# Expert 0 of a recurrent attention layer with a top-2 mixture of experts: four low halves made earlier, a third bank for turned rows, high and low halves in one tile, three scatters issued apart

## Chip, cores and metric

One core of a Trainium2 chip runs the whole program. The metric is the device time of one execution in microseconds (us), the median of three runs.

## What is computed

Four batches of eight heads and 768 steps go through a gated linear recurrence with a running maximum. Its output, 3072 rows of 320 numbers, is the input x of eight experts, of which each row goes to two:

```python
noisy_logits = x @ w_gate + log1p(exp(x @ w_noise)) * noise
top2_w = softmax over the two largest
for e in range(8):
    for k in range(2):
        mask = top2[:, k] == e
        h = np.maximum(x[mask] @ w1[e], 0.0)           # 320 -> 1024
        out[mask] += top2_w[mask, k, None] * (h @ w2[e])   # 1024 -> 320
```

## The kernel before

**Precision.** Each matrix is kept as a high half (rounded to fp32r) and a low half (what the rounding left). A product is three matmuls: high with high, high with low, low with high. W2H and W2L are the halves of an expert's second weights, HH and HLO those of the first product's result after the relu, XH and XL those of the turned rows.

**Stages.** The recurrence and the routing fill the first 131 us. Then expert 0 is computed while the routing of the last rows still runs on VectorE; its rows are dealt in three parts of 3, 2 and 2 tiles (tiles 0 to 2, 3 and 4, 5 and 6; tile 6 has 64 rows). After it come experts 1 to 7, with whole sets of tiles. For one expert the rows are gathered by POOL with indirect DMAs (gather, line 781), turned by TensorE for experts 0 and 1 (transpose_x, line 807: three transposes into one PSUM bank, then ACT copies to XH at line 813 and VectorE subtracts to XL and XH at lines 814 and 815), multiplied with the first weights (mm1, line 997), then with the second (mm2, line 1029), scaled by VectorE to a tile y, and added to the output in HBM by an indirect DMA of POOL (put, line 1055).

**Order of expert 0 (lines 1096 to 1162).** First product of part 0 in eight steps f, with routing work put in between by advance (line 1074); the low half of each step is held in the list `later` and issued at the end of advance. Then the second product of tiles 0 to 2 in three passes k (line 1113): HH with W2H, HLO with W2H, HH with W2L. In pass 1 VectorE makes the eight low halves W2L at line 1119; a decode and two gathers (rows of tiles 3 and 4) are issued early in pass 1; in pass 2 tiles 3 and 4 are turned. The three results are not scattered yet, they stay in `held`. Then the first product of part 1 (line 1133), in which the last decode and five gathers are issued (tiles 5 and 6 of expert 0, tiles 0 to 2 of expert 1); two more gathers (line 1141), the three held scatters (line 1143), and the second product of tiles 3 and 4 with five turns in between (tiles 5, 6 and, for expert 1, 0 in that of tile 3; tiles 1 and 2 in that of tile 4). Then the first product of part 2 (line 1149) with the turns of tiles 3 and 4 of expert 1 after its steps 0 and 3, and the second product of tiles 5 and 6.

**Banks.** bank (line 733) deals PSUM banks in turn: "h" for first products from s0, s1 and e, "x" for turned rows from s0 and s1, "y" for second products from st and o. s0 and s1 have two buffers each, e, st, o and xt one. A new tile waits for the readers of the one before it in its buffer. Each engine works its instructions in the order in which the program issues them.

**Tail columns.** Where a part has more than 768 columns, its last 64 (tile 6) go to a tile HT of their own: a relu at line 1026 and a low half at line 1027, after the relu and the low half of the other columns (lines 1016 and 1019). That is so for experts 0 to 4.

Of the kernel before, what the change touches and what calls it, by code (L numbers as in the profile page):

```python
# [7 lines left out]
F32 = mybir.dt.float32  # L8
FR = mybir.dt.float32r
# [55 lines left out]
def build(ctx, tc, qk, vk, og, fi, noise, wgn, w1, w2, cst, ce, out):  # L65
# [666 lines left out]

    def bank(use):

        n = dict(h=("s0", "s1", "e"), x=("s0", "s1"), y=("st", "o"))[use]
        turn[use] += 1
        name = n[turn[use] % len(n)]
        return psum.tile([128, 512], F32, name=name, bufs=2 if name in ("s0", "s1") else 1)
# [27 lines left out]
    def weigh(e, h=None):  # L766

        if not h:
            GW[e] = rt.tile([128, 7], F32, name="gw", bufs=2)
            GW[e, 2] = rt.tile([128, 7, 2], F32, name="gw2", bufs=2)  # L770
        t = tiles(e, h)
        n = slice(t[0], t[-1] + 1)
        V.tensor_mul(GW[e, 2][:, n], XG[:, n, DM:DM + 2], KM[:, TC * e + n.start:TC * e + n.stop])
        V.tensor_add(GW[e][:, n], GW[e, 2][:, n, 0], GW[e, 2][:, n, 1])
# [23 lines left out]
    def tiles(e, h=None):  # L798
        if h is None:
            return range(7 if is_long(e) else 6)  # L800
        c = parts(e)[h]
        return range(c.start // 128, -(-c.stop // 128))
# [154 lines left out]
    XTP = XTB[:, 0:384].rearrange("p (j t) -> p j t", j=3)  # L957
    m2 = ctx.enter_context(tc.tile_pool(name="m2", bufs=1, reuse_waits="tile"))
    RAW2 = m2.tile([128, 8, DM], F32, name="raw2")
    HH = m2.tile([128, 8, NM], FR, name="hh")  # L960
    HLO = m2.tile([128, 8, NM], FR, name="hlo")
    HT = m2.tile([128, 8, 128], FR, name="ht")
    XB = m2.tile([128, 12, 224], F32, name="xb")
    XT = m2.tile([128, 3, NT], F32, name="xt_")

# [31 lines left out]
    def mm1(e, h, f, later=None):  # L997
        c, s = parts(e)[h], slice(f * 128, f * 128 + 128)
        n = c.stop - c.start
        ps = bank("h")  # L1000
        hh = [(W1H[:, k, s], XH[:, k, c]) for k in range(2)]
        hl = [(W1H[:, k, s], XL[:, k, c]) for k in range(2)] + [(W1H[:, 2, s], XH[:, 2, c])]
        lh = [(W1L[:, k, s], XH[:, k, c]) for k in range(2)] + [(W1L[:, 2, s], XH[:, 2, c])]

        ops = hh + (hl + lh if e else lh + hl)
        for i, (l, r) in enumerate(ops):
            T.matmul(ps[:, 0:n], l, r, start=i == 0, stop=i == len(ops) - 1)  # L1007
        if e > 1:
            m = NM // 2
            x = ps[:, 0:m].rearrange("p (t x) -> p t x", x=64)  # L1010
            hi, lo = (a[:, f].rearrange("p (t h x) -> p h t x", h=2, x=64)[:, h] for a in (HH, HLO))
        else:
            c = slice(c.start, min(c.stop, NM))
            m = c.stop - c.start
            x, hi, lo = ps[:, 0:m], HH[:, f, c], HLO[:, f, c]
        A.activation(hi, x, AF.Relu)  # L1016

        def rest():
            V.scalar_tensor_tensor(lo, x, 0.0, hi.bitcast(F32), op0=OP.max, op1=OP.subtract)  # L1019

        if later is None:
            rest()
        else:
            later.append(rest)
        if m < n:
            A.activation(HT[:, f, 0:64], ps[:, m:n], AF.Relu)
            V.scalar_tensor_tensor(HT[:, f, 64:], ps[:, m:n], 0.0, HT[:, f, 0:64].bitcast(F32), op0=OP.max, op1=OP.subtract)

    def mm2(e, t, b="y", between={}):
        n = rows_of(t)  # L1030
        ps = bank(b)[:, 0:DM]
        y = m2.tile([128, DM], F32, name="y", bufs=TA + 1)
        if n == 128:
            c = slice(128 * t, 128 * t + 128)
            for j in range(8):
                T.matmul(ps, HH[:, j, c], W2H[:, j], start=j == 0, stop=False)  # L1036
                T.matmul(ps, HH[:, j, c], W2L[:, j], start=False, stop=False)  # L1037
                T.matmul(ps, HLO[:, j, c], W2H[:, j], start=False, stop=j == 7)  # L1038
                if j in between:
                    transpose_x(between[j])  # L1040
        else:

            for j in range(8):
                T.matmul(ps, HT[:, j], W2H[:, j], start=j == 0, stop=False)
                T.matmul(ps, HT[:, j], W2L[:, j], start=False, stop=j == 7)
            A.activation(y[0:n], ps[n:128], AF.Copy)
            V.tensor_add(y[0:n], y[0:n], ps[0:n])
            ps = y
        V.tensor_scalar(y[0:n], ps[0:n], GW[e][0:n, t:t + 1], None, op0=OP.mult)  # L1049
        return y  # L1050
# [4 lines left out]
    def put(e, t, y):  # L1055
        n = rows_of(t)

        P.memset(gap, 0.0)
        st = P.indirect_dma_start(out=out, out_offset=bass.IndirectOffsetOnAxis(ap=token(e, t), axis=0),  # L1059
                                  in_=y[0:n], in_offset=None, compute_op=OP.add)  # L1060
        for o in puts.setdefault(e, []):
            tc.declare_no_dep(st.ins, o.ins, reason="an expert has a token once")
        puts[e].append(st)
# [29 lines left out]

    unit[0] = NU
    weigh(0, 0)
    wipe = lambda: next(clear, None)
    lag[:] = 8, 11
    for f in range(8):
        mm1(0, 0, f, later)
        for _ in range(3):  # L1100
            wipe()
        A.activation(W2H[:, f], raw2[:, f], AF.Copy)
        if f == 0:
            logits(NU)
        if f == 1:
            t_part(NU - 1)
            tc_part(NU - 1)
        if f == 2:
            logits(NU + 1)
        advance(0.85, 4)  # L1110
    lag[:] = 10, 9
    sums = [bank("h")[:, 0:DM] for _ in tiles(0, 0)]
    for k, (l, r) in enumerate(((HH, W2H), (HLO, W2H), (HH, W2L))):
        for n in range(24):
            t, j = divmod(n, 8)
            T.matmul(sums[t], l[:, j, 128 * t:128 * t + 128], r[:, j], start=k == 0 and j == 0, stop=k == 2 and j == 7)
            if k == 1 and n % 2 == 0 and 6 <= n < 22:
                x = n // 2 - 3
                V.tensor_sub(W2L[:, x], raw2[:, x], W2H[:, x].bitcast(F32))
            if n % 2:  # L1120
                wipe()
                advance((0.27, 0.0, 0.27 if n < 14 else 0.0)[k])
            if k == 2 and j == 7:
                held[t] = m2.tile([128, DM], F32, name="y", bufs=TA + 1)
                A.activation(held[t], sums[t], AF.Copy, scale=GW[0][:, t:t + 1])
            if k == 2 and n in (14, 19):
                transpose_x(tiles(0, 1)[n // 19])
# [11 lines left out]
    dealing = deal()  # L1139
    load_w2(1)  # L1140
    gather(1, ts=tiles(0, 1))
    for t in held:
        put(0, t, held[t])
    for t in tiles(0, 1):
        put(0, t, mm2(0, t, "y", {0: 5, 3: 6, 6: 0} if t == 3 else {2: 1, 5: 2}))
    weigh(0, 2)
    gather(1, ts=tiles(0, 2))
    side = split_w1(V)
    for f in range(8):
        mm1(0, 2, f)  # L1150
        next(dealing, None)
        if f == 5:
            next(side)
        if f in (0, 3):
            transpose_x(tiles(0, 1)[f // 3])
    run(dealing)
    for t in tiles(0, 2):
        y = mm2(0, t)
# [212 lines left out]
```

## Time and profile before

| | us |
|---|---|
| median of 3 runs | 531.01 |
| all runs | 529.98, 531.01, 535.59 |
| profiled execution | 529.92 |
| its span, first to last instruction | 528.1 |
| PE (matmul) busy | 507.6 |
| DVE busy | 344.3 |
| ACT busy | 250.2 |
| POOL busy | 227.6 |

PE is TensorE's matmuls, PEld its weight loads, DVE is VectorE, ACT ScalarE, POOL GpSimd. The ends of matmuls are modelled and the next one starts before the last ends, so the step from start to start is what a matmul takes. In square brackets a row names the idle time of its engine before it and what ended it; "issue" is a wait for nothing that the profile shows.

### The profile page before, as it was taken

To read this page: it belongs to the slowest core of one execution; us is meant where nothing else is said; L and a number is where in the kernel's file an instruction comes from. 1 tells how busy PE (TensorE), PEld (TensorE's weight loads), DVE (VectorE), ACT (ScalarE), POOL (GpSimd) and SP (SyncE) were. 2 spreads that over 40 slices of the span, in tenths; PEclk is the share of its full clock that TensorE was granted. 3 is DMA by queue.
4 is the path that set the end of the run, shared out by engine and by line. 5 is a ranking of instruction groups with operands and counts; after the bars stand their busy time and mean duration, and the time that the engine had idled before them with its cause. 6 is when DMAs were issued, how large, how long until landed. Compare 5 with 4: busy or idle time off the path is not lost.

```text
span 528.1 us, 13192 instructions
## 1 busy us (share of the span) xinstructions
PE 507.6 (96%) x5052; PEld 476.8 (90%) x5053; DVE 344.3 (65%) x963; ACT 250.2 (47%) x607; POOL 227.6 (43%) x294
## 2 busy tenths in 40 slices
PE   9899989998999899999999999999999999999994
PEld 4688888887988797999999999999999999999994
DVE  7788989999887377763765485367448447545410
ACT  7688878889513145441533353054325315514300
POOL 7366575264012746245515623460553245141043
PEclk9699999999999899999999999999999999999998
DMA  5697786876767527059329515931862483272033
GB/s 163 185 273 238 218 230 187 230 223 209 256 191 238 96 40 204 18 116 261 87 53 271 101 38 107 262 91 37 235 119 61 102 256 87 59 169 25 2 38 41
DMA packets 52437, 76.80 MB, mean 145 GB/s; under 512 B 10809, under 2 KB 43072, under 8 KB 52368
## 3 DMA queue, kind: packets, MB, share of 16 engines
q1 hardware_dynamic: 40288, 53.20, 33.6%
q0 software_dynamic: 12080, 22.69, 21.3%
q8 instruction: 42, 0.69, 0.5%
q14 instruction: 27, 0.22, 0.1%
HBM read 52.27 MB, written 17.48 MB: 132 GB/s over the span
## 4 chain that ended last, share of the span: by engine, by line
PE 75%; DVE 14%; ACT 4%; issue 3%; POOL 2%; DMA 2%; SPq 0%; POOLq 0%; DVEq 0%
PE s L1007 23%; PE e L1007 11%; PE o L1037 5%; PE o L1036 5%; PE o L1038 5%; PE st L1037 5%; PE st L1036 5%; PE st L1038 5%; PE o L385 3%; DVE p L362 3%; PE s L348 2%; DVE ob L639 2%; PE e L325 2%; PE st L376 1%; DVE kd L356 1%
## 5 line engine op out<-in xcount | busy, mean ns | idle before, releaser
L1059 POOL DMA_INDIRECT y_out<-y,tok x53 | 87.2, 1645 | 191.9 <-DVE y L1049 190.8
L1016 ACT ACTIVATE hh<-s 128x384 fp32r<-128x384 f32 (+3 forms) x91 | 42.8, 470 | 89.7 <-PE s L1007 82.7
L1007 PE MATMUL s<-xh,w1h 128*128 128x384 f32 (+5 forms) x273 | 76.8, 338 | 0.7 <-DVE vc L462 0.7
L781 POOL DMA_INDIRECT xg<-rows,tok x53 | 60.0, 1133 | 28.3 <-issue 14.4
L1019 DVE SCALAR_TENSOR_TENSOR hlo<-s,hh 128x384 fp32r<-128x384 f32 (+3 forms) x91 | 47.8, 525 | 27.0 <-ACT hh L1016 23.3
L1007 PE MATMUL s<-xh,w1l 128*128 128x384 f32 (+5 forms) x273 | 62.4, 336 | 0.7 <-DVE xh L815 0.7
L1037 PE MATMUL o<-w2l,hh 128*128 128x320 f32 x184 | 57.3, 312 | 0.0
L1036 PE MATMUL o<-w2h,hh 128*128 128x320 f32 x184 | 57.2, 311 | 0.0
L1038 PE MATMUL o<-w2h,hlo 128*128 128x320 f32 x184 | 56.6, 307 | 0.0
L1036 PE MATMUL st<-w2h,hh 128*128 128x320 f32 x176 | 55.2, 313 | 0.4 <-issue 0.4
L1037 PE MATMUL st<-w2l,hh 128*128 128x320 f32 x176 | 55.4, 315 | 0.1
L1038 PE MATMUL st<-w2h,hlo 128*128 128x320 f32 x176 | 54.6, 310 | 0.4 <-issue 0.4
L1007 PEld LDWEIGHTS s<-xh,w1h 128*128 128x128 f32 x273 | 48.9, 188 | 2.6 <-PE s L1007 0.9
L1007 PEld LDWEIGHTS s<-xh,w1l 128*128 128x128 f32 x273 | 47.9, 188 | 2.3 <-DVE xh L815 0.9
L1007 PE MATMUL s<-xl,w1h 128*128 128x384 f32 (+5 forms) x182 | 46.3, 336 | 0.0
L1016 ACT ACTIVATE hh<-e 128x384 fp32r<-128x384 f32 (+3 forms) x45 | 21.3, 474 | 45.3 <-PE e L1007 43.1
L1049 DVE TENSOR_SCALAR y<-o,gw 128x320 f32<-128x320 f32 x23 | 12.6, 550 | 43.4 <-PE o L1038 43.4
L1049 DVE TENSOR_SCALAR y<-st,gw 128x320 f32<-128x320 f32 x22 | 12.1, 551 | 43.8 <-PE st L1038 43.7
L397 POOL TENSOR_TENSOR xr<-tm,vk 128x320 f32<-128x320 f32 x24 | 20.9, 871 | 42.2 <-ACT w L328 12.0
L1007 PE MATMUL e<-xh,w1h 128*128 128x384 f32 (+5 forms) x135 | 38.7, 340 | 0.1
L385 PE MATMUL o<-vk,p 104*64 104x41 f32 (+2 forms) x768 | 30.0, 237 | 5.2 <-DVE p L362 2.5
L1036 PEld LDWEIGHTS o<-w2h,hh 128*128 128x128 f32 x184 | 34.6, 188 | 0.2 <-DVE y L1049 0.2
(235 smaller groups left out, 1267.9 us busy)
## 6 DMA issues: line engine op xcount, KB each, us to landing
raw<-w_in SPq DMA_DIRECT2D x7, 1280.0 KB
raw<-w_in SPq DMA_DIRECT2D x7, 1024.0 KB
qk<-qk_in SPq DMA_DIRECT2D x24, 256.0 KB
raw<-w_in SPq DMA_DIRECT2D x19, 256.0 KB
y_out<-zrow SPq DMA_DIRECT2D x15, 320.0 KB
vk<-vk_in POOLq DMA_DIRECT2D x24, 162.0 KB
vk<-vk_in SPq DMA_DIRECT2D x24, 162.0 KB
vk<-og_in SPq DMA_DIRECT2D x24, 160.0 KB
```

The source lines that it names most:

```text
L362: V.tensor_mul(PP[u], SQ[u], W[u])
L385: T.matmul(OQ[u][half[p], h, :], PP[u][n, p, h, :], VK[u % 4][p][n, h * 41:h * 41 + 41], start=True, stop=True)
L397: P.tensor_mul(XR[u], tm.rearrange("p h d -> p (h d)"), SG[u % 4])
L781: P.indirect_dma_start(out=XG[0:rows_of(t), t], out_offset=None, in_=XD[0:n], in_offset=bass.IndirectOffsetOnAxis(ap=token(e, t), axis=0), ...
L1007: T.matmul(ps[:, 0:n], l, r, start=i == 0, stop=i == len(ops) - 1)
L1016: A.activation(hi, x, AF.Relu)
L1019: V.scalar_tensor_tensor(lo, x, 0.0, hi.bitcast(F32), op0=OP.max, op1=OP.subtract)
L1036: T.matmul(ps, HH[:, j, c], W2H[:, j], start=j == 0, stop=False)
L1037: T.matmul(ps, HH[:, j, c], W2L[:, j], start=False, stop=False)
L1038: T.matmul(ps, HLO[:, j, c], W2H[:, j], start=False, stop=j == 7)
L1049: V.tensor_scalar(y[0:n], ps[0:n], GW[e][0:n, t:t + 1], None, op0=OP.mult)
L1059: st = P.indirect_dma_start(out=out, out_offset=bass.IndirectOffsetOnAxis(ap=token(e, t), axis=0), in_=y[0:n], in_offset=None, compute_op= ...
```

## The change

Four edits. (1) The low halves W2L of the chunks 0 to 3 are appended to `later` in steps 4 to 7 of expert 0's first product, those of the chunks 4 to 7 are issued in pass 1 at n = 4, 8, 12, 16 (before: all eight, at n = 6 to 20). (2) Turned rows get their bank from xt, s0, xt, s1 in turn in place of s0, s1. (3) HH, HT and HLO become views of one tile HX, so that the high half of the tail columns lies right behind HH: one relu writes both, and the low half of the tail follows that of the other columns. This holds for all experts. (4) Of the held scatters, tile 0's is issued before the second product of tile 3, tile 1's before that of tile 4, tile 2's after step 1 of the first product of part 2. The two turns in that product move from steps 0 and 3 to steps 2 and 4.

```diff
-        n = dict(h=("s0", "s1", "e"), x=("s0", "s1"), y=("st", "o"))[use]
+        n = dict(h=("s0", "s1", "e"), x=("xt", "s0", "xt", "s1"), y=("st", "o"))[use]
...
-    HH = m2.tile([128, 8, NM], FR, name="hh")
-    HLO = m2.tile([128, 8, NM], FR, name="hlo")
-    HT = m2.tile([128, 8, 128], FR, name="ht")
+    HX = m2.tile([128, 8, 2 * NT], FR, name="hx")
+    HH, HT, HLO = HX[:, :, 0:NT], HX[:, :, NM:NT + CS], HX[:, :, NT + CS:]
...
+            hi, lo = HH[:, f, c], HLO[:, f, c.start:c.start + m]
+            top = x[:, 0:m], hi[:, 0:m]
         A.activation(hi, x, AF.Relu)
 
         def rest():
-            V.scalar_tensor_tensor(lo, x, 0.0, hi.bitcast(F32), op0=OP.max, op1=OP.subtract)
+            V.scalar_tensor_tensor(lo, top[0], 0.0, top[1].bitcast(F32), op0=OP.max, op1=OP.subtract)
+            if m < n:
+                V.scalar_tensor_tensor(HT[:, f, CS:], ps[:, m:n], 0.0, HT[:, f, 0:CS].bitcast(F32), op0=OP.max, op1=OP.subtract)
...
-        if m < n:
-            A.activation(HT[:, f, 0:64], ps[:, m:n], AF.Relu)
-            V.scalar_tensor_tensor(HT[:, f, 64:], ps[:, m:n], 0.0, HT[:, f, 0:64].bitcast(F32), op0=OP.max, op1=OP.subtract)
...
+    def low_w2(x):
+        V.tensor_sub(W2L[:, x], raw2[:, x], W2H[:, x].bitcast(F32))
...
         A.activation(W2H[:, f], raw2[:, f], AF.Copy)
+        if f > 3:
+            later.append(lambda x=f - 4: low_w2(x))
...
-            if k == 1 and n % 2 == 0 and 6 <= n < 22:
-                x = n // 2 - 3
-                V.tensor_sub(W2L[:, x], raw2[:, x], W2H[:, x].bitcast(F32))
+            if k == 1 and n % 4 == 0 and 4 <= n < 20:
+                low_w2(n // 4 + 3)
...
-    for t in held:
-        put(0, t, held[t])
     for t in tiles(0, 1):
+        put(0, t - 3, held[t - 3])
         put(0, t, mm2(0, t, "y", {0: 5, 3: 6, 6: 0} if t == 3 else {2: 1, 5: 2}))
...
+        if f == 1:
+            put(0, 2, held[2])
         if f == 5:
             next(side)
-        if f in (0, 3):
-            transpose_x(tiles(0, 1)[f // 3])
+        if f in (2, 4):
+            transpose_x(tiles(0, 1)[f // 4])
```

## Rows read from the trace of the kernel before

**Rows 1.** Stages of the span: the first column is the stretch in us from the span's start, then its length, the busy time and (instructions) of PE, PEld, DVE, ACT and POOL, the granted clock of TensorE (1.00 is its upper level), the DMA engines' share and GB/s.

```profile
146.30:160.70 14.40, 14.18 (x92) 11.83 (x90) 13.85 (x69) 3.19 (x8) 2.61 (x3) 1.00 0.64 200
...
169.50:182.90 13.40, 11.85 (x65) 9.93 (x64) 3.05 (x9) 2.47 (x6) 10.20 (x12) 0.88 0.51 99
182.90:192.00 9.10, 8.27 (x72) 7.99 (x72) 7.30 (x28) 3.05 (x14) 5.42 (x6) 0.99 0.44 66
...
200.00:224.00 24.00, 24.00 (x130) 21.15 (x129) 17.75 (x47) 11.82 (x30) 10.89 (x15) 1.00 0.39 116
...
477.00:500.00 23.00, 23.00 (x134) 23.00 (x134) 12.23 (x25) 10.86 (x24) 1.67 (x2) 1.00 0.09 13
```

**Rows 2.** The timeline of the end of the first product of part 0 and the start of the second (start, duration, engine, line, operation, out<-in, count, idle time before).

```profile
143.48 0.19 DVE L540 SCALAR_TENSOR_TENSOR co<-t,ue 128x32 f32<-128x32 f32 x1 [0.18 <-ACT t L701]
...
145.98 0.23 DVE L601 TENSOR_SCALAR rk<-rk,bump 128x4 f32<-128x4 f32 x1 [0.82 <-ACT rk L509]
...
149.07 1.42 DVE L639 TENSOR_SCALAR ob<-spot,bi,cs 128x128 f16<-128x128 f16 x6
149.20 1.19 PEld L1116 LDWEIGHTS e<-w2h,hh 128*128 128x128 f32 x8 [0.38 <-DVE hlo L1019]
...
150.78 0.27 PEld L448 LDWEIGHTS <-ob 128*128 128x128 f16 x8
```

**Rows 3.** The same timeline where passes 1 and 2 meet: the eight low halves, the matmuls that wait for them, and the gather of tile 4.

```profile
153.92 3.29 DVE L1119 TENSOR_TENSOR w2l<-raw,w2h 128x320 fp32r<-128x320 f32 x8
...
154.74 3.97 PE L1116 MATMUL s<-w2l,hh 128*128 128x320 f32 x15
...
155.61 1.29 POOL L781 DMA_INDIRECT xg<-rows,tok  x1 [0.30 <-issue]
155.66 0.19 PEld L1116 LDWEIGHTS s<-w2l,hh 128*128 128x128 f32 x1 [0.21 <-DVE w2l L1119]
```

**Rows 4.** The same timeline at the end of pass 2: the turn of tile 4 on PE, its last low half on DVE, and the matmul of the next first product that waits for that.

```profile
159.61 0.49 PE L811 MATMUL s<-cs,xg 128*128 128x128 f32 x3
...
161.74 0.29 DVE L815 TENSOR_TENSOR xh<-s,xh 64x128 fp32r<-64x128 f32 x1
...
162.08 0.39 PE L1007 MATMUL s<-xh,w1l 128*128 128x256 f32 x1 [0.66 <-DVE xh L815]
```

**Rows 5.** PE's timeline in the second product of tiles 3 and 4: its first two matmuls, the turn of tile 5 and the matmul behind it, the turn of tile 6, a matmul after a gap, and the last two.

```profile
169.50 0.31 PE L1036 MATMUL o<-w2h,hh 128*128 128x320 f32 x1
169.64 0.31 PE L1037 MATMUL o<-w2l,hh 128*128 128x320 f32 x1
...
170.02 0.52 PE L811 MATMUL s<-cs,xg 128*128 128x128 f32 x3
170.29 0.39 PE L1036 MATMUL o<-w2h,hh 128*128 128x320 f32 x1
...
171.79 0.40 PE L811 MATMUL s<-cs,xg 64*128 64x64 f32 x3
...
179.74 0.62 PE L1036 MATMUL st<-w2h,hh 128*128 128x320 f32 x1 [0.40 <-issue]
...
182.39 0.47 PE L1037 MATMUL st<-w2l,hh 128*128 128x320 f32 x1
182.66 0.47 PE L1038 MATMUL st<-w2h,hlo 128*128 128x320 f32 x1
```

**Rows 6.** ACT's timeline in the same stretch: the copies of the turned tiles 5 and 6, then DVE's last step on tile 6, then ACT's copies of tiles 0 to 2, three in one row.

```profile
174.03 0.49 ACT L813 ACTIVATE xh<-s 128x384 fp32r<-128x384 f32 x1 [2.44 <-PE s L811]
...
178.34 0.33 ACT L813 ACTIVATE xh<-s 128x192 fp32r<-128x192 f32 x1 [3.82 <-PE s L811]
...
179.01 0.23 DVE L815 TENSOR_TENSOR xh<-s,xh 64x64 fp32r<-64x64 f32 x1
...
181.24 1.25 ACT L813 ACTIVATE xh<-s 128x384 fp32r<-128x384 f32 x3 [2.56 <-remote]
```

**Rows 7.** POOL's timeline in the same stretch: the last of seven gathers, the first and the last of the three held scatters, the scatter of tile 3, and the second of the two gathers behind that of tile 4.

```profile
174.68 1.01 POOL L781 DMA_INDIRECT xg<-rows,tok  x1 [0.30 <-issue]
...
175.99 1.64 POOL L1059 DMA_INDIRECT y_out<-y,tok  x1 [0.19 <-issue]
...
179.81 1.55 POOL L1059 DMA_INDIRECT y_out<-y,tok  x1 [0.19 <-issue]
...
183.35 1.55 POOL L1059 DMA_INDIRECT y_out<-y,tok  x1 [1.86 <-DVE y L1049]
...
188.57 1.00 POOL L781 DMA_INDIRECT xg<-rows,tok  x1 [0.30 <-PE s L1007]
```

**Rows 8.** The first product of part 2: the wait of ACT's tail relu in 182.9 to 192 us (total, times, longest), the low half, tail relu and tail low half of step 0, the first matmul of step 5 after its gap, and the first of the second product behind step 7.

```profile
ACT ht L1026 <- DVE hlo L1019: 3.2, 4, 1.2
...
185.23 0.28 DVE L1019 SCALAR_TENSOR_TENSOR hlo<-e,hh 128x128 fp32r<-128x128 f32 x1
185.55 0.23 ACT L1026 ACTIVATE ht<-e 128x64 fp32r<-128x64 f32 x1 [1.24 <-DVE hlo L1019]
...
185.81 0.22 DVE L1027 SCALAR_TENSOR_TENSOR ht<-e,ht 128x64 fp32r<-128x64 f32 x1 [0.29 <-ACT ht L1026]
...
189.23 0.44 PE L1007 MATMUL s<-xh,w1h 128*128 128x192 f32 x2 [0.74 <-DVE vc L462]
...
191.96 0.33 PE L1036 MATMUL o<-w2h,hh 128*128 128x320 f32 x1
```

More of the change, by code (lines that the diff above doesn't have):

```diff
@@ L1007, in mm1 @@
             T.matmul(ps[:, 0:n], l, r, start=i == 0, stop=i == len(ops) - 1)
+        m = NM // 2 if e > 1 else min(c.stop, NM) - c.start
+        x = ps[:, 0:n]
         if e > 1:
-            m = NM // 2
-            x = ps[:, 0:m].rearrange("p (t x) -> p t x", x=64)
-            hi, lo = (a[:, f].rearrange("p (t h x) -> p h t x", h=2, x=64)[:, h] for a in (HH, HLO))
-        else:
-            c = slice(c.start, min(c.stop, NM))
-            m = c.stop - c.start
-            x, hi, lo = ps[:, 0:m], HH[:, f, c], HLO[:, f, c]
+            x = x.rearrange("p (t x) -> p t x", x=CS)
+            hi = HH[:, f].rearrange("p (t x) -> p t x", x=CS)[:, h:h + 2 * (n // CS) - 1:2]
+            lo = HLO[:, f].rearrange("p (t h x) -> p h t x", h=2, x=CS)[:, h]
+            top = x[:, 0:m // CS], hi[:, 0:m // CS]
+        else:
+            hi, lo = HH[:, f, c], HLO[:, f, c.start:c.start + m]
+            top = x[:, 0:m], hi[:, 0:m]
         A.activation(hi, x, AF.Relu)
         def rest():
-            V.scalar_tensor_tensor(lo, x, 0.0, hi.bitcast(F32), op0=OP.max, op1=OP.subtract)
+            V.scalar_tensor_tensor(lo, top[0], 0.0, top[1].bitcast(F32), op0=OP.max, op1=OP.subtract)
+            if m < n:
+                V.scalar_tensor_tensor(HT[:, f, CS:], ps[:, m:n], 0.0, HT[:, f, 0:CS].bitcast(F32), op0=OP.max, op1=OP.subtract)
         if later is None:
```

## The prediction

> **What bounds the kernel now.** I read the stages of the span first [rows 1]. From 200 to 500 us PE is busy in all of every stretch (the rows show the first and the last of 13): experts 1 to 7 are bound by matmuls that the change doesn't touch, so a shorter tail relu there frees ACT and DVE time that nothing waits for, and I count nothing for it. What can move lies between 146 and 192 us, in expert 0: there PE's row shows gaps, one stage has a granted clock of 0.88, and in the first stage DVE is busy 13.85 of 14.40 us, so it is DVE's order that sets the end there. Then I read the timelines of these stages, for what each engine waits for.
>
> In 146 to 160.7 us DVE makes the eight low halves in one block after the decode, and PE's matmuls of pass 2 come at their pace: each waits about 0.2 us for one [rows 3]. DVE is late by as much behind them, and the next first product waits 0.66 us for the low half of turned tile 4 [rows 4].
>
> In 169.5 to 182.9 us two second products and five turns take 13.4 us [rows 1]. From start to start a matmul takes 0.147 us (169.50 to 169.64) and a turn 0.27 (170.02 to 170.29) [rows 5]: 48 x 0.147 + 5 x 0.25 = 8.3 us, so 5.1 us are lost. The reader is to see that ACT copies turned tile 5 at 174.03 though its turn started at 170.02, tile 6 at 178.34 though its turn started at 171.79, and tiles 0 to 2 together at 181.24 [rows 5, 6]. In the later part PE's matmuls come with gaps that the profile calls issue, and the last run at 0.27 us a step [rows 5], the lower clock level. The three held scatters follow seven gathers without a pause; ACT catches up in the third scatter, which ends at 181.36 [rows 6, 7]. That is a coincidence in time; no row says that one delays the other.
>
> In 182.9 to 192 us eight steps of a first product and two turns take 9.1 us. A step without a gap is 0.91 us (steps 5 to 7 from 189.23 to 191.96), so 8 x 0.91 + 2 x 0.25 = 7.8 us, and 1.3 are lost, most of it ahead of 189.23, where step 5 waits for its bank [rows 1, 8].
>
> **Low halves sooner.** One takes 3.29 / 8 = 0.41 us [rows 3]. Four of them, 1.64 us, move ahead of the decode. DVE had idle time of 0.18 and 0.82 us in steps 4 to 6 [rows 2]; the first moved one fills 0.18 and the second fits in the 0.82 with what the first left over. The third and fourth find none and push what is behind them by 0.82 us: the low half of step 7, on which the bank of the third sum waits (PE goes at 149.20), the OB operands that the burst's weight loads at 150.78 need [rows 2], the decode, and behind it the two gathers. So pass 1 ends some 0.6 us later (between 0.41 and 0.82, as some of it hides in PE's order). Pass 2 no longer waits: from about 155.35, 24 x 0.147 + 2 x 0.25 = 4.0 us, it could end at 159.4 in place of 160.68. What is late next is the gather of tile 4: issued at 156.4, not 155.61. It was landed by 159.61, when the tile was turned [rows 3, 4], so it is landed at the latest 4.0 us after its start, at 160.4; if it had landed earlier than its turn, the new turn is at 159.6 or before. From the turn the chain is 1.75 us: 0.49 each for the turn and its copy, and some 0.8 for two DVE steps, of which the second takes 0.29 [rows 4, 6]. The first product then goes on at 161.35 to 162.2 in place of 162.08: between +0.7 and -0.1, I take **0.5 us gained**. The block behind it, DVE's OB work, ends 0.8 us sooner and doesn't hold this. The weight loads behind the low halves on SP's queue start up to 0.9 us earlier, are needed 30 us later, and meet the two gathers more; that is in the lower bound.
>
> **One tile for both halves.** Before, the tail relu waits for the low half of the other columns (3.2 us in four times), so one step goes through ACT, DVE, ACT and DVE: 185.23 to 186.03 from the first low half on [rows 8]. After, a relu over 192 columns is followed by two DVE steps, 0.28 + 0.22 us; eight instructions of ACT fall away in this stage. The bank comes free about 0.3 us sooner a step, and a turn's copy no longer stands behind a tail relu on ACT's queue.
>
> **Another bank, turns moved.** With the new turn of banks, steps 1, 4 and 5 of this product get buffers that turns 0 and 2 or part 1 left, and step 5 doesn't wait for step 2. Of the 1.3 us I take **1.2 gained** with the edit above; the rest stays in bank e, which has one buffer and is dealt to steps 0, 3 and 6. Bounds 0.5 and 1.3. The other side of this edit is in the stage before: xt has one buffer, and tiles 4, 6 and 1 get it one after another. So the turn of tile 1 now waits until DVE is done with tile 6, which was at 179.24 (179.01 + 0.23) [rows 6]; before, it had a buffer of its own.
>
> **Scatters apart.** Tile 0's scatter keeps its place. Behind it POOL now waits for tile 3's y, behind that come tile 1, tile 4, two gathers and tile 2. POOL gets later by two scatters, 3.7 us (179.81 - 175.99 is two of them [rows 7]), and with it the two gathers behind tile 4's, which ended at 189.57 [rows 7]. Their rows are turned after the second product of tile 5, which starts at 191.96 [rows 8] and takes 24 x 0.147 = 3.5 us; so gathers that end at 193.3 are hidden, with 1 to 2 us to spare for their landing. If the burst of scatters is what holds up PE and ACT, they catch up when the first ends, near 177.6: tile 6 is done at about 178, tile 1 is turned then, and what is left, 15 matmuls and two turns, 15 x 0.147 + 2 x 0.25 = 2.7 us, ends at 180.7, 2.2 us gained. If not, tile 1 waits until 179.24, and the same rest ends at 181.9 at the upper clock level: 1.0 gained, since PE's scattered matmuls of 177 to 180.5 then run in one piece. At the lower level (0.27 a step) it takes 5.0 us and ends at 184.2: 1.3 lost. If everything that was lost goes, 5.1 are gained. I take **1.5 us gained**, between the first two, which are the nearest to the rows.
>
> A rule that speaks against the change bears on this. The clock was granted at 0.88 in this stage [rows 1], and PE had worked with gaps before it fell. The Trainium skill (TensorE: Matmul & The Clock Gate, HAM oscillation — how this bites in real kernels) says that a wait of PE for data can put its clock back to half rate, with the work behind the wait starting cold. By it the waiting turn would cost the 1.3 us above and the sum would be 529.5; by the trace, where the gaps were longer before the clock fell, it is 526.7.
>
> **Sum.** 0.5 + 1.2 + 1.5 = 3.2 us off the profiled execution's 529.92 gives **526.7 us**. That execution lies 1.1 us under the median of 531.01, within the spread of the three runs. A change under 1% (5.3 us) can't be told from none here.
>
> **Rivals.** (a) The delay in 169.5 to 182.9 us goes altogether, since it needs ten indirect DMAs without a pause: 0.5 + 5.1 + 1.3 = 6.9, so 523.0. For it speaks that ACT follows its turns at once where POOL is quiet (159.61 to 160.14 of tile 4); against it that tile 5's copy was already 3.5 us late before the first scatter [rows 6, 7], and the gathers stay. (b) The one buffer of xt takes the place of the burst: tile 6 is read as late as before or later, PE stands until then, and the clock falls. At the old 178.34 this costs 1.3 us, and every us later costs one more; with 1.2 gained behind it and nothing in front, the kernel is slower than before from 178.5 on. With a read one us later it is 529.92 + 2.3 - 1.2 = 531.0; with one at 181.24, as the last three had, 532.9. Against it speaks that the two later scatters are away then. (c) The stage is what it was, since neither scatters nor banks set it: only 0.5 and 1.2 count, 528.2.
>
> **How the numbers follow.** The forecast has 0.45, (a) 0.22, (b) 0.18, (c) 0.15. Under the forecast the time is 525 to 529 by the bounds of its terms. The range reaches from (a) at 523.0 to (b) at 531.0: 522.5 to 531.5, which leaves out the later reads of (b) and about 0.1 on the other side. Faster by over 1% than the median is below 525.7: (a) and a little of the forecast, 0.28. Slower by over 1% needs over 536.3, which only a long wait of (b), or DVE's pushed chain together with it, could give: 0.04. Within 1%: 0.68.
>
> **What would show it.** Pass 2 in one piece without waits for W2L, ending near 159.5 to 160.2; the stall ahead of the first product of part 1 shorter but not gone; ACT's copies of tiles 5 and 6 still late, those of 0 to 2 no longer in one row at 181; the turn of tile 1 behind DVE's last step on tile 6; 169.5 to 182.9 shorter by 1 to 2 us; no gap before step 5 of part 2's product; 24.00 of 24.00 as before from 200 us on. I am wrong if POOL's scatters have no bearing on ACT's late copies, if tile 1's wait for its bank lasts over 3 us, or if the later decode makes the gathers of tiles 3 and 4 the new wait.

## The result and the profile after

The changed kernel takes 534.75 us (median of 20 runs, 529.54 to 540.01) against 531.75 for the one before, measured beside it: a ratio of 1.0053, with a 95% interval of 1.0028 to 1.0078, so some 2.8 us slower (3.0 by the two medians). That is within the 1% named ahead, but on the other side of the forecast, and above its range. The profiled execution takes 534.53 us, its span is 532.8.

Each stage runs from its first matmul to the first matmul of the next. Here are two traces of each kernel, the second ones from the experiments below.

| us | before | before, again | after | after, again |
|---|---|---|---|---|
| first product of expert 0 starts at | 132.99 | 133.47 | 136.30 | 133.05 |
| first product of part 0 | 13.38 | 13.49 | 13.48 | 13.46 |
| three passes | 14.31 | 14.31 | 18.93 | 19.19 |
| first product of part 1 | 8.82 | 8.88 | 9.11 | 9.38 |
| second product of tiles 3, 4 | 13.42 | 11.19 | 11.30 | 10.48 |
| first product of part 2 | 9.04 | 10.08 | 7.75 | 7.75 |
| second product of tiles 5, 6 | 6.65 | 6.67 | 6.66 | 6.66 |
| experts 1 to 7 and end | 329.44 | 329.47 | 329.23 | 329.45 |
| from the first product to the end | 395.1 | 394.1 | 396.5 | 396.4 |

The program up to 133 us is the same in both kernels and takes a different time in each execution, so I compare by stages. From the first product on, the changed kernel loses 1.3 to 2.4 us: 4.6 to 4.9 in the passes, 0.2 to 0.6 behind them, and in the two stages after that it gets back up to 2.9 (in one of the four pairings of these traces it loses 0.1) and 1.3 to 2.3.

The stages of the changed kernel in the view that [rows 1] show of before (same columns):

```profile
149.78:168.71 18.93, 13.56 (x91) 12.33 (x90) 13.93 (x69) 3.19 (x8) 2.33 (x3) 0.90 0.73 225
168.71:177.82 9.11, 9.11 (x73) 9.07 (x73) 5.82 (x31) 3.23 (x8) 2.07 (x3) 0.84 0.28 89
177.82:189.12 11.30, 9.12 (x65) 8.55 (x64) 3.71 (x11) 2.58 (x6) 7.08 (x9) 1.00 0.41 92
189.12:196.87 7.75, 7.75 (x73) 7.75 (x71) 7.26 (x30) 3.83 (x10) 6.77 (x8) 1.00 0.63 83
200.00:224.00 24.00, 24.00 (x128) 20.84 (x128) 18.86 (x47) 12.33 (x27) 12.73 (x17) 1.00 0.47 126
```

PE is busy 13.56 us in the passes, somewhat less than the 14.18 of before, in a stage that is 4.6 us longer: it stands. The timeline of the changed kernel shows where, with the loads of expert 1's weights on SP's queue:

```profile
158.13 1.69 DVE L1098 TENSOR_TENSOR w2l<-raw,w2h 128x320 fp32r<-128x320 f32 x4
158.42 1.10 POOL L781 DMA_INDIRECT xg<-rows,tok  x1 [0.88 <-DVE km L479]
...
158.96 2.37 PE L1122 MATMUL s<-w2l,hx 128*128 128x320 f32 x15
159.49 0.38 SPq L153 DMA_DIRECT2D raw<-w_in  x1
159.82 1.01 POOL L781 DMA_INDIRECT xg<-rows,tok  x1 [0.30 <-issue]
159.97 1.12 SPq L150 DMA_DIRECT2D raw<-w_in  x2
...
161.57 0.55 PE L811 MATMUL s<-cs,xg 128*128 128x128 f32 x3 [0.24 <-DMA xg<-rows,tok]
...
166.94 0.90 PE L811 MATMUL xt<-cs,xg 128*128 128x128 f32 x3 [4.09 <-DMA xg<-rows,tok]
...
168.71 0.63 PE L1006 MATMUL s<-xh,w1h 128*128 128x256 f32 x2
```

Four low halves follow the decode (158.13), not eight, and PE's matmuls of pass 2 come in one row without waiting for one (158.96). But the low halves are the readers of the tile into which expert 1's weights are loaded. So the third of the four, done at about 159.4 (158.13 and three of 0.42), lets the load of line 153 start, 0.33 us ahead of the gather of tile 4 (159.82). The chain of waits names what follows (start, duration):

```profile
159.82 7.07 DMA xg<-rows,tok
```

Before, the same load was issued 1.27 us behind that gather: 156.88 in its timeline, against 155.61 [rows 3], and PE turned tile 4 at 159.61 [rows 4].

```profile
156.88 0.38 SPq L153 DMA_DIRECT2D raw<-w_in  x1
```

The DMA queues of the changed kernel in 161.5 to 162.5, 162.5 to 163.5 and 164.5 to 165.5 us (q0 is POOL's queue, q1 SP's; packets, MB, share of the 16 engines):

```profile
q1 hardware_dynamic: 94, 0.39, 100.2%
...
q1 hardware_dynamic: 100, 0.41, 100.6%
...
q0 software_dynamic: 35, 0.14, 63.6%
q1 hardware_dynamic: 34, 0.08, 35.6%
```

For two us the engines carry nothing but the load; the gather's packets come after it. By 163.5 us the load has moved 0.91 of its 1.05 MB (0.11 MB in the us before these windows, then 0.39 and 0.41). Before, in 157 to 158 and 158 to 159 us, the gather went first:

```profile
q0 software_dynamic: 17, 0.09, 43.6%
...
q1 hardware_dynamic: 28, 0.11, 68.5%
q0 software_dynamic: 31, 0.07, 18.2%
```

A lead at the issue is not yet a lead at the engines. In the 18 traces the first packet of a gather of tile 3 or 4 that nothing held up comes 1.7 to 2.0 us after its issue, and the first of the load 1.0 to 1.4 us after its own. Of the 1.27 us before, about half a us was left: the gather's first packet is at 157.59, the load's at 158.09.

In the second product of tiles 3 and 4 the timeline answers to [rows 5 to 7]:

```profile
178.26 0.51 PE L811 MATMUL s<-cs,xg 128*128 128x128 f32 x3
...
180.03 0.40 PE L811 MATMUL xt<-cs,xg 64*128 64x64 f32 x3
...
180.92 0.49 ACT L813 ACTIVATE xh<-s 128x384 fp32r<-128x384 f32 x1 [1.10 <-PE xt L811]
...
185.24 0.33 ACT L813 ACTIVATE xh<-xt 128x192 fp32r<-128x192 f32 x1 [3.82 <-remote]
...
185.91 0.23 DVE L815 TENSOR_TENSOR xh<-xt,xh 64x64 fp32r<-64x64 f32 x1
...
186.23 0.52 PE L811 MATMUL xt<-cs,xg 128*128 128x128 f32 x3 [2.18 <-ACT xh L813]
```

ACT copies tile 6 at 185.24, 5.2 us after its turn began. The turn of tile 1 waits for xt until DVE is done with tile 6 (186.14; the row names ACT's copy, but that ended at 185.57), as rival (b) has it, but at a clock of 1.00.

### The profile page after: what moved, and what is told of

It reads as the page before. It is cut to its first block, busy times and chain, and to the rows that moved or that the text cites. A ratio compares the mean times of both kernels' runs of the same rounds, so it can differ in the third digit from the quotient of the medians.

```text
span 532.8 us, 13159 instructions
## 1 busy us (share of the span) xinstructions
PE 504.4 (95%) x5052; PEld 477.5 (90%) x5053; DVE 340.1 (64%) x963; ACT 247.4 (46%) x567; POOL 225.2 (42%) x294
## 4 chain that ended last, share of the span: by engine, by line
PE 79%; DVE 10%; DMA 4%; issue 2%; ACT 2%; POOL 1%; another core or an unknown queue 1%; SPq 1%; POOLq 0%; DVEq 0%
PE s L1006 24%; PE e L1006 12%; PE o L1037 5%; PE o L1036 5%; PE o L1038 5%; PE st L1037 5%; PE st L1036 5%; PE st L1038 5%; PE o L385 3%; PE s L348 2%; DMA xg<-rows,tok 2%; DVE p L362 2%; PE st L376 2%; PE e L325 1%; PE xt L428 1%
## 5 line engine op out<-in xcount | busy, mean ns | idle before, releaser
L1017 ACT ACTIVATE hx<-s 128x384 fp32r<-128x384 f32 (+5 forms) x91 | 44.4, 488 | 109.2 <-PE s L1006 65.0
L1020 DVE SCALAR_TENSOR_TENSOR hx<-s,hx 128x384 fp32r<-128x384 f32 (+3 forms) x91 | 48.2, 529 | 38.2 <-ACT hx L1017 30.8
L781 POOL DMA_INDIRECT xg<-rows,tok x53 | 57.5, 1085 | 32.7 <-issue 14.4
L1037 PE MATMUL o<-w2l,hx 128*128 128x320 f32 x184 | 57.3, 312 | 0.0
L1036 PE MATMUL o<-w2h,hx 128*128 128x320 f32 x184 | 57.1, 310 | 0.0
L1038 PE MATMUL o<-w2h,hx 128*128 128x320 f32 x184 | 56.6, 308 | 0.0
L1037 PE MATMUL st<-w2l,hx 128*128 128x320 f32 x176 | 54.9, 312 | 0.0
L1036 PE MATMUL st<-w2h,hx 128*128 128x320 f32 x176 | 54.5, 310 | 0.0
L1038 PE MATMUL st<-w2h,hx 128*128 128x320 f32 x176 | 54.1, 307 | 0.0
L1017 ACT ACTIVATE hx<-e 128x384 fp32r<-128x384 f32 (+5 forms) x45 | 22.1, 491 | 52.9 <-PE e L1006 34.1
L385 PE MATMUL o<-vk,p 128*64 128x41 f32 (+2 forms) x768 | 30.0, 235 | 6.2 <-issue 2.9
L1038 PEld LDWEIGHTS o<-w2h,hx 128*128 128x128 f32 x184 | 34.7, 188 | 0.0
```

The costliest lines, as they stand in the source:

```text
L385: T.matmul(OQ[u][half[p], h, :], PP[u][n, p, h, :], VK[u % 4][p][n, h * 41:h * 41 + 41], start=True, stop=True)
L781: P.indirect_dma_start(out=XG[0:rows_of(t), t], out_offset=None, in_=XD[0:n], in_offset=bass.IndirectOffsetOnAxis(ap=token(e, t), axis=0), ...
L1020: V.scalar_tensor_tensor(lo, top[0], 0.0, top[1].bitcast(F32), op0=OP.max, op1=OP.subtract)
```

## The experiments

Theory A: the loads that the early low halves release go ahead of the gather of tile 4 and hold it up. Rivals: edits 2 to 4 cost the time (B), DVE's later decode does (C). The kernels of one group ran on the same chip, those of different groups on different ones, save that groups 2 and 4 share one. Stages in us as above; the ratio is to the kernel before, and a kernel without one was executed once, in its trace.

| group, kernel | passes | part 1 | tiles 3, 4 | part 2 | to the end | ratio (95%) |
|---|---|---|---|---|---|---|
| 1, e1 | 14.31 | 8.82 | 11.99 | 7.74 | 392.2 | 1.0008 (0.9985 to 1.0032) |
| 1, e2 | 14.16 | 8.26 | 13.57 | 7.74 | 393.1 | 0.9967 (0.9932 to 1.0003) |
| 1, e3 | 19.20 | 9.64 | 12.04 | 9.78 | 400.1 | 1.0139 (1.0102 to 1.0176) |
| 1, e4 | 14.18 | 8.20 | 13.70 | 8.14 | 393.9 | 1.0014 (0.9988 to 1.0040) |
| 2, before again | 14.31 | 8.88 | 11.19 | 10.08 | 394.1 | 1.0012 (0.9983 to 1.0040) |
| 2, e5 | 14.14 | 8.37 | 11.22 | 7.75 | 390.8 | 0.9945 (0.9909 to 0.9981) |
| 2, e6 | 14.30 | 8.83 | 9.01 | 7.74 | 388.8 | |
| 2, e8 | 14.32 | 8.81 | 10.36 | 7.88 | 390.8 | |
| 3, e8 again | 14.31 | 8.83 | 10.59 | 7.77 | 390.9 | 0.9945 (0.9914 to 0.9976) |
| 3, e9 | 14.16 | 8.33 | 10.71 | 7.75 | 390.3 | 0.9932 (0.9901 to 0.9962) |
| 3, e10 | 19.15 | 8.54 | 11.28 | 7.74 | 396.1 | |
| 3, e7 | 14.33 | 8.82 | 12.22 | 8.29 | 393.0 | |
| 4, after again | 19.19 | 9.38 | 10.48 | 7.75 | 396.4 | |
| 4, e11 | 21.21 | 8.76 | 11.19 | 7.74 | 398.3 | |
| 5, e12 | 16.75 | 8.17 | 8.94 | 7.74 | 390.9 | |
| 5, e7 again | 14.33 | 8.82 | 9.09 | 7.74 | 389.3 | |

**e1: low halves as before.**

```diff
...
-        if f > 3:
-            later.append(lambda x=f - 4: low_w2(x))
...
-            if k == 1 and n % 4 == 0 and 4 <= n < 20:
-                low_w2(n // 4 + 3)
+            if k == 1 and n % 2 == 0 and 6 <= n < 22:
+                x = n // 2 - 3
+                V.tensor_sub(W2L[:, x], raw2[:, x], W2H[:, x].bitcast(F32))
```

> The changed kernel with edit 1 undone: all eight low halves W2L in pass 1 at n = 6 to 20 again, edits 2 to 4 kept. Theory A (the gather of tile 4 is overtaken by the weight loads that the last low half releases on SP's queue): the loads start after the gather again, the gather of tile 4 lands in about 3 us, the turn of tile 4 doesn't wait 4.09 us, the first product of part 1 starts 14 to 14.5 us after the first matmul of the three passes (18.9 in the changed kernel, 14.3 before), and the gains of the later stages stay (2.1 in the second product of tiles 3 and 4, 1.3 in the first product of part 2): 3 to 3.5 us under the kernel before, ratio about 0.994. Rival B (edits 2 to 4 cost the time): no better than the changed kernel, ratio about 1.005.

The stages came as theory A has them: the load is again 1.27 us behind the gather (161.19 and 159.92), tile 4 is turned without a wait, the passes take 14.31 us and the whole from the first product on 392.2, 2.9 or 1.9 less than in the two traces of before. B falls. The ratio of 1.0008 is a miss: the first product started at 137.20 in its trace, and the stages explain only what lies behind that.

**e2: early low halves, loads held back.** A DMA of 4 bytes reads the gathered rows of tile 4 into a tile of its own, GATE (declared elsewhere), so it waits for that gather; the loads stand behind it on SP's queue.

```diff
-    load_w1(1)
+    SP.dma_start(GATE[0:1, 0:1], XG[0:1, 4, 0:1]); load_w1(1)
```

> The changed kernel with all four edits, and ahead of the loads of expert 1's first weights a 4-byte DMA on SP's queue that reads the gathered rows of tile 4, so that the loads start only when that gather has landed. Theory A: the gather of tile 4 lands in about 3 us after its issue, the passes end 0.5 us earlier than before (about 13.8 us after their first matmul), and the kernel is 3.5 to 4 us under the one before, ratio about 0.993. Rival C (DVE's pushed chain, the later decode, costs the time, and the loads nothing): the gather is late all the same, ratio about 1.005.

Its timeline, with the turns of tiles 3, 4 and 5:

```profile
160.49 0.55 PE L811 MATMUL s<-cs,xg 128*128 128x128 f32 x3 [0.16 <-DMA xg<-rows,tok]
...
161.81 0.55 PE L811 MATMUL xt<-cs,xg 128*128 128x128 f32 x3
161.82 0.67 SPq L1135 DMA_DIRECT2D gate<-xg  x1
...
162.61 0.40 SPq L153 DMA_DIRECT2D raw<-w_in  x1
...
174.81 0.52 PE L811 MATMUL s<-cs,xg 128*128 128x128 f32 x3 [3.01 <-DMA xg<-rows,tok]
```

The gather of tile 4 was issued at 158.83 and its tile turned at 161.81, 2.98 us later; the decode was as late as in the changed kernel. So C falls, and A holds for this stage. But the loads, now 162.6 and later, meet the gather of tile 5 (issued at 168.52), and PE waits 3.01 us for that one. The conflict had moved, which I had not expected, and the gain is less than expected: 0.9967, with 1 inside the interval.

**e3 and e4: edit 1 alone in the kernel before, without and with the loads held back.**

```diff
...
         A.activation(W2H[:, f], raw2[:, f], AF.Copy)
+        if f > 3:
+            later.append(lambda x=f - 4: low_w2(x))
...
-            if k == 1 and n % 2 == 0 and 6 <= n < 22:
-                x = n // 2 - 3
-                V.tensor_sub(W2L[:, x], raw2[:, x], W2H[:, x].bitcast(F32))
+            if k == 1 and n % 4 == 0 and 4 <= n < 20:
+                low_w2(n // 4 + 3)
```

> The kernel before with edit 1 alone. Theory A: the gather of tile 4 takes about 7 us, the passes take some 4.6 us longer than before, the next product starts at half clock, and nothing is gained behind: 4.5 to 5 us over the kernel before, ratio about 1.009. Rival B: 0.5 us gained, ratio about 0.999. In case the order of gather and loads falls out differently from run to run: between the two, with runs of both kinds.

> The kernel before with edit 1 and the 4-byte DMA ahead of the loads, as in e2. Theory A: only what the prediction gave to the low halves is left, 0.5 us gained (0.1 lost to 0.7 gained), ratio 0.999. Rival C: as edit 1 alone, ratio about 1.009.

Edit 1 alone makes the passes 4.9 us longer, with a wait of 4.38 us for the gather of tile 4, and the kernel slower at a ratio of 1.0139, more than expected. With the loads held back, passes and part 1's product take 22.38 us together, 0.75 less than before: that is what the early low halves are worth with the loads out of the way (no run holds the loads back without them). PE then waits 3.13 us for tile 5, as in e2, and the ratio is 1.0014, no difference that can be told.

**before_again: the kernel before against itself.**

> The kernel before, unchanged, against itself: how far a ratio of 1 can be told here, and a second trace. Theory A: the stages from 146 us on last as long as in its first trace (14.3, 8.8, 13.4 and 9.0 us), and only the recurrence in front of them, 133.0 us to the first product of expert 0 in that trace and 135.3 to 138.8 in the five traces of changed kernels, differs between executions; ratio 1.000 with about 0.003 to each side. Rival D: the recurrence is always about 133 us in this kernel, and the changed kernels lose 2 us there in a way not seen; then this trace shows 133 again.

A ratio of 1.0012 with 0.003 to each side. The second product of tiles 3 and 4 takes 11.19 us where the first trace has 13.42, and the product behind it 10.08 instead of 9.04: these stages are not fixed. In the first trace the granted clock fell at 179.58, inside the first of these two stages (0.88 over the stage, [rows 1]); in the second it stayed at 1.00 through both. The start at 133.47 again leaves rival D open; against it, e8 started at 132.95 and 133.35 and the second trace of the changed kernel at 133.05. For it speaks that seven of the eight changed kernels that were timed come out 0.7 to 2.8 us worse by their ratio than by the stages of their traces, set against the mean of the two traces of before; only e2 doesn't. For most of them the difference is inside the interval.

**e5: both loads held back.**

```diff
-    load_w2(1)
+    SP.dma_start(GATE[0:1, 0:1], XG[0:1, 2, 0:1]); load_w2(1)
```

> As e2 (all four edits, the loads of expert 1's first weights behind the gather of tile 4), and a second 4-byte DMA that holds the load of its second weights until the gather of tile 2 of expert 1, the last of the seven, has landed. In e2 the gather of tile 5 was issued while the loads still ran and PE waited 3.01 us for it; with half of the bytes gone from that stretch theory A expects that wait to be under 0.5 us, the second product of tiles 3 and 4 to take 11 to 12 us (13.57 in e2, 11.99 in e1), and the whole 1.5 to 2.5 us less than e2: ratio to the kernel before about 0.993. Rival E (the wait for tile 5 comes of the gather's own queue, not of the loads): 13.5 us as in e2, ratio about 0.997.

No wait for tile 5 is left, the second product of tiles 3 and 4 takes 11.22 us, and the kernel is faster than the one before at 0.9945. So E falls.

**e10: the first load ahead of the gather, the second held back.** The diff is that of e5 on the changed kernel.

> The changed kernel with only the second 4-byte DMA of e5: the load of expert 1's first weights (1.5 MB) is issued ahead of the gather of tile 4 as in the changed kernel, the load of its second weights (1.25 MB) waits for the seventh gather. Theory A as a matter of bytes: with 1.5 of 2.75 MB left the gather of tile 4 lands 2.5 to 3.5 us earlier than in the changed kernel, some 4 us after its issue (7.07 there), and the three passes take 15.5 to 16.5 us (18.93 there, 14.3 before). Rival H (the gather stands behind the loads' first transfer, however much follows): 18 to 19 us as in the changed kernel.

Rival H is what came: 19.15 us, with the gather of tile 4 issued at 160.25 and its tile turned at 167.59, after the same 4 us of wait. The 1.25 MB of the second weights don't matter.

```profile
167.59 0.90 PE L811 MATMUL xt<-cs,xg 128*128 128x128 f32 x3 [4.20 <-DMA xg<-rows,tok]
```

**e11, e12: the first load in four pieces, from the front and from the end.**

```diff
-    load_w1(1)
+    [SP.dma_start(RAW1[:, k, s:s + 512], w1[1, 128 * k:128 * k + 128, s:s + 512]) for k in (1, 0) for s in (512, 0)]; load_w1(1, (2,))
```

This is e12; e11 has (0, 1) and (0, 512).

> The changed kernel with the 1024 KB load ahead of the gather of tile 4 issued as four loads of 256 KB, same bytes, same place on SP's queue. Theory A1 (the DMA engines take turns between the queues, but only from one transfer to the next, so that the gather stands behind the large load as a whole): the gather gets its turn after one piece or two, lands 1.5 to 2.5 us earlier than in the changed kernel, and the three passes take 16.5 to 17.5 us (18.93 there, 19.15 in e10). Rival A2 (what was queued first goes first, in any number of pieces): 18.5 to 19.5 us.

> As e11, with the four pieces in the opposite order, so that the first one needs the low half of chunk 6 and none is issued before the one large load of the changed kernel would be (in e11 the pieces started ahead of the gather of tile 3 too). Theory A1 (the DMA engines take turns between the queues from one transfer to the next): the gather of tile 4 gets its turn after a piece or two, PE's wait for it is 1.5 to 3 us instead of 4.1, and the three passes take 16.5 to 18 us. Rival A2 (turns or not, the gather shares the engines until the 1.5 MB are through): 18.5 to 19.5 us.

e11 answered another question: its first piece needs only low halves that are ready early, so it went ahead of the gather of tile 3 too, and PE waited 3.65 us for that and 2.96 for the next. In e12 the first piece is again 0.33 us ahead of the gather of tile 4, as the large load was, and PE waits 2.48 us, not 4.1. The timeline's turn, and the queues in 160 to 161 and 161 to 162 us:

```profile
162.77 0.55 PE L811 MATMUL xt<-cs,xg 128*128 128x128 f32 x3 [2.48 <-DMA xg<-rows,tok]
```

```profile
q1 hardware_dynamic: 91, 0.17, 61.9%
q0 software_dynamic: 22, 0.09, 32.6%
...
q1 hardware_dynamic: 115, 0.21, 65.8%
q0 software_dynamic: 24, 0.08, 24.0%
```

Now both queues move in the same us, as A1 has it. But the pieces also come in packets half as long (2 KB in place of 4 KB), so it stays open whether the number of loads or the length of their packets lets the gather in. The Trainium skill (DMA: Bandwidth & Descriptors, Queues, rings and completion order) says that each DMA engine takes turns between its queues, changing only when it has drained a whole packet (by that page a bundle of descriptors, so not one of the packets that the views count). That agrees with e12, and with a large load as one long turn in the changed kernel; how long a turn was, no run here shows.

**e6: two gathers in the row instead of seven.** It starts from e1 and leaves out five gathers of expert 1.

```diff
                 if h == 2:
-                    gather(1, ts=tiles(0, 0))
+                    pass
...
-    gather(1, ts=tiles(0, 1))
```

> e1 (low halves as before, edits 2 to 4) without the five gathers of expert 1's tiles 0 to 4, so that POOL issues two gathers in a row instead of seven ahead of the held scatter; expert 1 computes with the rows that stood there. Theory F (a long run of indirect DMAs on POOL holds up what ACT gets from PE): ACT copies the turned tiles 5 and 6 within 1 us of their turns (2.4 and 5.6 us in e1), the turn of tile 1 doesn't wait for bank xt (2.56 us in e1), and the second product of tiles 3 and 4 takes 8.5 to 9.5 us instead of 11.99. Rival G (POOL has nothing to do with it): 11.5 to 12 us, the copies as late as in e1.

It came as theory F has it: 9.01 us, and no wait of PE for xt; the copy of tile 5 is 1.14 us behind its turn, a little more than expected. This is one trace; the five others of this chip with seven gathers took 10.36 to 11.22 us. The turns and copies of tiles 5 and 6 in its timeline:

```profile
174.39 0.52 PE L811 MATMUL s<-cs,xg 128*128 128x128 f32 x3
...
175.53 0.49 ACT L813 ACTIVATE xh<-s 128x384 fp32r<-128x384 f32 x1 [0.36 <-PE s L811]
...
176.16 0.40 PE L811 MATMUL xt<-cs,xg 64*128 64x64 f32 x3
...
176.59 0.33 ACT L813 ACTIVATE xh<-xt 128x192 fp32r<-128x192 f32 x1 [0.57 <-PE xt L811]
```

**e7, e8: scatters together, and turns in s0 and s1.** Both start from e1. e8 has the old banks; e7 is e8 with the scatters as before.

```diff
-        n = dict(h=("s0", "s1", "e"), x=("xt", "s0", "xt", "s1"), y=("st", "o"))[use]
+        n = dict(h=("s0", "s1", "e"), x=("s0", "s1"), y=("st", "o"))[use]
```

> e1 with the turned rows in s0 and s1 alone, as before the change; scatters apart, one tile for both halves, turns after steps 2 and 4. If the wait for the single buffer of xt is a cost by itself: the 2.56 us ahead of the turn of tile 1 go, and the second product of tiles 3 and 4 takes 9.5 to 10.5 us (11.99 in e1). If that wait only stands where PE would lose the time anyway: 12 to 13.4 us. In the first product of part 2 the step that gets a turn's buffer waits again: 8 to 9 us, against 7.74 in e1.

> e8 timed: low halves and turned rows' banks as before the change, the other edits kept. By the stages of its first trace, 390.75 us from the first product of expert 0 to the end against 395.1 and 394.1 in the two traces of the kernel before: 3.9 us less, ratio 0.9927, if the recurrence in front takes the same time. If the recurrence is some 2 us longer in every changed kernel, as the ratio of e1 would have it: 0.996 to 0.997.

> e8 (low halves and turned rows' banks as before; one tile for both halves, turns after steps 2 and 4) with the three held scatters in a row ahead of the second product of tile 3, as before: only edit 4 apart from e8. If the two later scatters hold up what ACT gets from PE: the copies of tiles 0 to 2 come in the third scatter, as in the kernel before, and the second product of tiles 3 and 4 takes 11.2 to 13.4 us (10.36 in e8). If only the seven gathers matter: 10.3 to 10.7 us. The first product of part 2 stays at 7.7 to 7.9 us either way.

> e7 (scatters together) a second time, since this stage took 13.42 and 11.19 us in two traces of the kernel before, and 10.36 and 10.59 in two of e8. If edit 4 is worth something in it: over 11 us again (12.22 in e7). If not: 10.3 to 10.8 us, as in e8.

The stage takes 10.36 us in e8 and 11.22 in e5, of the same chip; 10.59 and 10.71 in e8 and e9 and 11.28 in e10 of another. By these pairs (which differ in the loads too) the wait for xt costs 0.6 to 0.9; but the second trace of the changed kernel, of e8's chip, has 10.48 with a wait of 1.33 us, so the cost is 0.1 to 0.9, not the whole wait. Part 2's product needs the third bank hardly at all (7.88 and 7.77, where I expected 8 to 9). e8 is faster than before at 0.9945. With the scatters together the stage took 12.22 us on the chip on which e8 took 10.59: 1.6 for edit 4 by one pair of traces, of which a part is the clock, 0.91 over the stage in e7 and 1.00 in e8; part 2's product took 8.29, more than expected. The second trace of e7, on another chip, has 9.09, under both values expected, with all seven gathers and three scatters in one run, and there ACT copied tile 6 0.43 us after its turn:

```profile
174.07 0.40 PE L811 MATMUL s<-cs,xg 64*128 64x64 f32 x3
...
174.50 0.33 ACT L813 ACTIVATE xh<-s 128x192 fp32r<-128x192 f32 x1 [1.17 <-PE s L811]
```

e12, of the same group, has 8.94. And in e2 and e4, on the chip of e1, tile 5 was turned among the seven gathers (in e2 at 174.81, with the gathers issued from 168.52 to 176.39) and copied 0.56 us later. So if F holds, it needs a second condition which these executions didn't meet, and e7 gives edit 4 no size that holds everywhere.

**e9: the parts together.** All four edits with both loads held back, turns in s0 and s1.

> e5 (early low halves, both loads held back) with the turned rows in s0 and s1 alone, as in e8. Theory: the parts add, passes 14.15 us, first product of part 1 8.35, second product of tiles 3 and 4 10.4, first product of part 2 7.8 to 7.9: 390.1 us from the first product of expert 0 to the end, 4.5 under the kernel before, ratio 0.9915 with a recurrence of the same length, 0.995 with one that is 2 us longer. If the early low halves bring nothing but their risk: as e8.

390.3 us from the first product on, 0.9932 of the kernel before: faster than both. Its lead over e8 again (0.6 us by the stages) is less than the intervals can tell.

**after_again: the changed kernel a second time.**

> The changed kernel a second time, for its stages: by theory A the three passes take 18.5 to 19.5 us again with a wait of PE for the gather of tile 4 of 3.5 to 4.5 us, the second product of tiles 3 and 4 takes 11 to 12 us, the first product of part 2 7.7 to 7.8. If the order in which loads and gather reach the DMA engines varies from execution to execution, the passes take 14 to 15 us in this one.

The wait came again, 4.18 us, and the passes took 19.19. The load was again 0.33 us ahead of the gather (156.23 and 156.56). The second product of tiles 3 and 4, at 10.48, took less than I expected. That execution took 531.2 us because its first product started at 133.05 and not at 136.30.

## Why the prediction was wrong

**The step that failed** is the last sentence of the low halves' part: the loads "start up to 0.9 us earlier, are needed 30 us later, and meet the two gathers more; that is in the lower bound". I priced the loads by when they are needed, and put the gathers' delay at no more than 0.6. With it fell the bound that the gather of tile 4 is landed "at the latest 4.0 us after its start": it took 7.07 to its use. The delay is 4.1 to 4.4 us of standing PE, and in both traces and e3 0.2 to 0.8 us in the first product behind it, whose stage has a granted clock of 0.84 in the first trace (in e10 it took 8.54, no longer than before). e3 shows it by that edit alone, e1, e2, e5 and e9 show it gone. Both numbers that decide were there: the gather 0.8 us later, the loads 0.9 earlier. The lead of the gather was 1.27, and 1.27 - 0.8 - 0.9 is below nothing; from the start of the passes on both shifts measured 0.80, which leaves -0.33. I gave each shift its own price and never subtracted them. The last sign of being wrong that I had named, the gathers as the new wait, came true, but by the loads: in e2, with the same late decode, the wait for tile 4 is gone.

**The rest of that part was right.** PE doesn't wait in pass 2; DVE's pushed order makes pass 2 start 0.81 us later from the start of the passes (I had 0.6, 0.82 at most); and 0.75 us are gained where the loads are out of the way (e4); I had 0.5, with 0.7 as the upper bound.

**One tile, banks and turns** in part 2's product: 1.3 us off the first trace of before, 1.2 predicted; against the second trace it is 2.3. No gap is left ahead of step 5. By e8 most of this comes without the third bank. And e4, which has none of these edits, takes 8.14 us here, behind a stage in which PE had waited for tile 5 and ACT copied tiles 5 and 6 within 1 us of their turns. So how much of the 1.3 is due to the edits isn't shown, and that it met the 1.2 is in part luck.

**Scatters apart and xt** in the second product of tiles 3 and 4: 2.1 us off the first trace, 1.5 predicted, but this stage varies by 2.2 us in the kernel before, and the first trace is the one in which the clock fell. ACT was still late on tiles 5 and 6, and the last three copies no longer came in one row, as forecast. Rival (b)'s wait is there (2.18 us). Its price was not: the clock stayed at 1.00, where (b) had it fall. Behind the wait of 4.09 us it did fall: the next stage has 0.84. The rule of the Trainium skill that I had weighed (TensorE: Matmul & The Clock Gate, HAM oscillation — how this bites in real kernels) agrees with the trace behind that wait; behind the one of 2.18 us nothing of it shows. My ground for a clock that stays up, that the gaps had been longer before it fell, was misread: in the trace of before PE is busy 2.12 of the 3.38 us from 176.20 to 179.58, where the clock fell, so it stood 1.26 us in all, in short gaps, against 2.18 in one piece here. By those rows it was luck that the clock stayed up. (Two small slips changed nothing: two scatters are 3.82 us, not 3.7, and by the sum of rival (b) the kernel is slower from 178.2, not 178.5.)

**Rival (a)**, that the delay goes if POOL's run is broken up, fits e6, which makes the run shorter, by one trace; the scatters alone didn't do it. **Rival (c)** is neither shown nor excluded, given the spread.

**The sum.** With the first trace's stages, 2.1 + 1.3 gained less 4.6 + 0.3 lost is 1.5 us slower by stages, at the edge of the measured 1.5 to 4.1. The difference to 2.8 lies ahead of the first product (rival D) or in the spread, and no run here tells which.

## What to carry to other kernels

When work is moved that frees a buffer, write down what the freed buffer lets start, and subtract: lead of the small urgent transfer, less its own delay, less the advance of the large one. Count it where the transfers start to move, not at their issue: here the gather takes 0.3 to 1.0 us longer than the load from issue to first packet (an estimate from the 1.7 to 2.0 and 1.0 to 1.4 us above; no run has a lead between -0.33 and 1.27). If the lead doesn't cover that, hold the large one back with something that waits for the small one, and look at the next small one in line too. Where one stage varies by more than the gain sought, compare stages over several traces, and on one chip.

## What the runs showed that was not expected

- A gather issued 0.33 us behind a 1024 KB load was 7.07 us from issue to use, against some 3.0 where it was ahead (e2). In four pieces of the same bytes, the wait fell from about 4.2 to 2.48 us.
- With seven gathers in a row on POOL, ACT's copies of turned tile 6 start 4.4 to 6.6 us behind the turn in the traces of e1, e3, e5, e8 to e11, the first of e7 and both kernels, and with two in a row 0.43 (e6). In the two traces of group 5 they start within 0.7 us in spite of the seven, and in e2 and e4, where PE came to tile 6 only when the last of the seven was issued, after 1.51 and 0.91. What sets the two apart, and what ACT waits for there, stays open.
- The same program ahead of the first product of expert 0 took 132.95 to 138.75 us in 18 traces. The cause wasn't tried.
